# Moving transposes from TensorE to DMA in an attention and SwiGLU kernel: queries and keys of the later eight pairs, and outputs from the seventh tile on

## The chip, the cores and the metric

The kernel runs on one core of one Trainium2 chip. The metric is device time in microseconds (us), as the median of several executions. The profile is a trace of one execution; its span is about 2 us shorter than the time, because it begins with the first instruction and ends with the last. The engines are PE (TensorE matmul), PEld (its weight loads), DVE (VectorE), ACT (ScalarE), POOL (GpSimd) and SP (SyncE, which here only issues DMAs; its lines in a trace read SPq).

## The reference

Attention over 4 batches, 8 heads, 768 positions and 64 dimensions. Three heads (0, 2, 6) are causal; five see only a window of 64 positions and 4 sink positions. A SwiGLU block on 3072 rows of 512 follows.

```python
scores = scale * np.matmul(q, k.transpose(0, 1, 3, 2))
stream_keep = causal & (is_sink | in_win)
scores = np.where(mask[None, :, :, :], scores, -1000000000.0)
a = np.exp(scores - max);  a = a / (sum(a) + 1e-09)
attn_out = np.matmul(a, v)
# ...
x = attn_out.transpose(0, 2, 1, 3).reshape(B * S, H * D)     # 3072 x 512
g = x @ w_gate                                               # 512 x 1536
silu = g * (1.0 / (1.0 + np.exp(-g)))
return (silu * (x @ w_val)) @ w_out                          # 1536 x 512
```

## The kernel before

The 3072 rows are 24 tiles of 128; two tiles in succession make a "pair", for which 256 positions of q, k and v are loaded in three DMAs of 512 KB. There are twelve pairs, 0 to 11. Four tiles make a "group" for the SwiGLU block, six in all. While PE runs the gate and value matmuls of one group, it runs the attention of the next in between, so the block gives PE steady work and the attention must be ready in time.

Everything is cast to 16 bits by ACT, DVE or POOL. Scores need the head dimension on the partitions, so queries and keys are transposed by PE against an identity, into PSUM, and copied out; the attention output `xb` goes the same way into `xt`, and from tile 12 on by a DMA.

```python
RINGS = {"raw": 11, "hq": 2, "e": 7, "xb": 3, "xt": 2, "sig": 2, "sil": 3, ...}   # buffers
XBAR = 12

def cast(n, kd, j):                       # q or k of pair n, one half of the positions
    ...
    copy(T_c[n, kd, j], hqs[n][:, "qk".index(kd), j]..., r[:, :, j]...)

def transposes(n, w):                     # w = 0: queries, 1: keys; 8 matmuls each
    ...
    for j in range(2):
        for p in range(4):
            nc.tensor.transpose(tr[...], hqs[n][:, w, j, p // 2, ...], ident)

def evack(n, x, ps):                      # PSUM -> SBUF
    copy(T_ev[n, 2][x], kT[b % 2][:, ps, pi * 256:(pi + 1) * 256], trs[n, 1][:, ps]...)

def xtranspose(t):
    if t >= XBAR:
        nc.sync.dma_start_transpose(out=xts[g][:, :, n * 128:(n + 1) * 128], in_=xb...)
        return
    # ... else four PE transposes and a copy
```

Each piece of work is a task. Two long strings, `ORDER` and `WAYS`, fix the order of all tasks and the engine of each; every engine, and the sync queue as well, runs its own list strictly in that order. An instruction that is not ready therefore holds up everything behind it on its engine. All loads and DMA transposes, and all stores but the last, are issued by the sync queue.

The softmax here doesn't subtract the row's maximum and nothing guards it: scores larger than these inputs give would overflow.

## Time and profile before

| | before |
|---|---|
| time | 271.59 us (271.56 to 271.64, 4 runs) |
| span, mean granted PE clock | 269.7 us, 1.000 |
| first gate matmul of group 2 starts | 73.5 us |
| last matmul ends | 265.1 us |
| DMA moved on the main queues | 36.05 MB |

The page cuts the span into 40 slices of 6.7 us and prints the busy share of each in tenths.

```profile
PE   7799889899999999999999999999999999999993
PEclk9999999999999999999999999999999999999999
DMA  7999999999950999011114210102014220110144
```

PE is full from the ninth slice on, its clock was never lowered, and the DMA engines are 90% busy or more only in slices 2 to 11 and 14 to 16. Two groups of instructions on the page are what the change acts on: the PE transposes of queries and keys, and the DMA transposes of outputs at the page's end (2.4 us from issue to landing).

```profile
L413 PE MATMUL tr<-ident,hq 128*128 128x128 f16 x192 | 15.0, 219 | 2.1 <-DVE m L264 1.0
```

The columns are busy us and mean ns of one, then the engine's idle time before them. The 219 ns includes the pipeline; in a row they start every 56 ns.

### The profile page before, as it was taken

Reading aid. Unit: us, or ns where it says so; the run is one execution under the profiler, and the core shown is the slowest. Engines: PE = TensorE matmul, PEld = TensorE weight load, DVE = VectorE, ACT = ScalarE, POOL = GpSimd, SP = SyncE. Lnnn points to the kernel's source line nnn. Section 1 sums busy time; section 2 is a strip of 40 time slices with the busy share of each in tenths; the row PEclk is TensorE's granted clock in tenths of the full one; section 3 lists DMA queues with packets and bytes.
Section 4 is the critical chain, followed back from the end, with each engine's and each line's share of the span. In section 5 each row is a group of like instructions: output and inputs, shape, how many; then the busy total and the mean of one; then the engine's idle time right before and its main releaser. Section 6 shows DMA issues by size and latency. Waiting matters only on the chain.

```text
span 269.7 us, 5353 instructions
## 1 busy us (share of the span) xinstructions
PE 257.9 (96%) x2063; PEld 150.2 (56%) x2063; DVE 173.6 (64%) x340; ACT 167.1 (62%) x260; POOL 113.0 (42%) x145
## 2 busy tenths in 40 slices
PE   7799889899999999999999999999999999999993
PEld 7777546465655565455566655555555554444441
DVE  6757787896679487666668257764582565555321
ACT  2499779999897668767757974486564613141300
POOL 6679936774786541876523233366320200000000
PEclk9999999999999999999999999999999999999999
DMA  7999999999950999011114210102014220110144
GB/s 193 295 347 349 332 280 357 341 288 290 289 158 11 256 310 277 8 40 41 39 21 98 61 39 19 41 19 62 1 23 96 59 59 3 39 39 0 41 102 93
DMA packets 55801, 36.52 MB, mean 135 GB/s; under 512 B 8160, under 2 KB 51168, under 8 KB 55776
## 3 DMA queue, kind: packets, MB, share of 16 engines
q1 hardware_dynamic: 55696, 36.05, 50.4%
q8 instruction: 16, 0.26, 0.4%
q10 hardware_dynamic: 80, 0.13, 0.2%
q14 instruction: 9, 0.07, 0.1%
HBM read 28.31 MB, written 6.29 MB: 128 GB/s over the span
## 4 chain that ended last, share of the span: by engine, by line
PE 80%; ACT 12%; DVE 5%; issue 2%; ACTq 0%
PE gv L761 42%; PE o_ps L790 21%; PE sc L524 9%; PE av L557 5%; ACT e L540 4%; PE tr L413 3%; ACT v L178 2%; ACT hq L178 2%; ACT sig L767 1%; ACT vt L178 1%; DVE m L264 1%; PE xtr L582 1%; DVE v L290 1%; DVE k L289 1%; DVE wg_sb L180 1%
## 5 line engine op out<-in xcount | busy, mean ns | idle before, releaser
L540 ACT ACTIVATE e<-sc 128x1024 f16<-128x1024 f32 (+4 forms) x67 | 60.9, 909 | 22.9 <-PE sc L524 22.5
L761 PE MATMUL gv<-xt,wg_sb 128*128 128x512 f16 (+1 forms) x304 | 71.7, 368 | 1.7 <-DVE wg_sb L180 1.2
L761 PE MATMUL gv<-xt,wv_sb 128*128 128x512 f16 (+1 forms) x304 | 72.3, 368 | 0.0
L548 POOL TENSOR_TENSOR e<-e,m 128x640 f16<-128x640 f16 (+1 forms) x25 | 44.5, 1787 | 66.0 <-ACT e L540 65.9
L790 PE MATMUL o_ps<-wo_sb,h 128*128 128x512 f16 x288 | 71.8, 379 | 0.3 <-ACT o_sb L178 0.3
L767 ACT ACTIVATE sig<-gv 128x512 f32<-128x512 f32 (+1 forms) x76 | 43.1, 575 | 44.6 <-PE gv L761 42.6
L771 DVE SCALAR_TENSOR_TENSOR sil<-sig,gv 128x512 f32<-128x512 f32 (+1 forms) x76 | 49.5, 656 | 31.6 <-ACT sig L767 31.1
L778 DVE SCALAR_TENSOR_TENSOR h<-sil,gv 128x512 f16<-128x512 f32 (+1 forms) x76 | 48.8, 655 | 9.6 <-PE gv L761 8.5
L761 PEld LDWEIGHTS <-wg_sb 128*128 128x128 f16 x304 | 28.9, 98 | 29.3 <-DVE wg_sb L180 1.4
L761 PEld LDWEIGHTS <-wv_sb 128*128 128x128 f16 x304 | 28.7, 98 | 26.6 <-issue 0.2
L790 PEld LDWEIGHTS <-h 128*128 128x128 f16 x288 | 26.6, 98 | 26.3 <-issue 0.5
L524 PE MATMUL sc<-qT,kT 128*128 128x256 f16 (+1 forms) x228 | 35.2, 257 | 1.4 <-ACT e L540 0.8
L180 POOL COPY v<-vt 32x528 f16<-32x528 f16 (+1 forms) x46 | 29.4, 639 | 6.5 <-ACT vt L178 3.8
L524 PEld LDWEIGHTS <-kT 128*128 128x128 f16 x228 | 20.6, 98 | 13.3 <-issue 2.7
L180 POOL CAST vt<-raw 64x512 f16<-64x512 f32 x30 | 18.6, 623 | 16.1 <-DMA raw<-in_v_dram 11.2
L557 PEld LDWEIGHTS <-e 128*128 128x128 f16 x472 | 20.1, 97 | 7.5 <-issue 0.5
L565 DVE RECIPROCAL rc<-av 128x4 f32<-128x4 f32 x48 | 8.6, 180 | 24.0 <-PE av L557 23.6
L178 ACT CAST hq<-raw 128x512 f16<-128x512 f32 x32 | 19.3, 617 | 4.3 <-DMA raw<-in_q_dram 3.0
L557 PE MATMUL av<-vt,e 128*128 128x65 f16 x392 | 21.7, 193 | 0.2 <-DVE xb L566 0.2
L566 DVE TENSOR_TENSOR xb<-av,rc 128x256 f16<-128x256 f32 x48 | 20.4, 424 | 1.7
L413 PE MATMUL tr<-ident,hq 128*128 128x128 f16 x192 | 15.0, 219 | 2.1 <-DVE m L264 1.0
L413 PEld LDWEIGHTS <-hq 128*128 128x128 f16 x192 | 12.2, 98 | 5.7 <-DVE m L264 1.2
(57 smaller groups left out, 191.8 us busy)
## 6 DMA issues: line engine op xcount, KB each, us to landing
raw<-in_q_dram SPq DMA_DIRECT2D x12, 512.0 KB, 7.2
raw<-in_k_dram SPq DMA_DIRECT2D x12, 512.0 KB, 7.1
raw<-in_v_dram SPq DMA_DIRECT2D x12, 512.0 KB, 7.4
out_dram<-o_sb SPq DMA_DIRECT2D x47, 128.0 KB, 2.3
raw<-in_moe_w_gate_dram SPq DMA_DIRECT2D x6, 512.0 KB, 8.7
raw<-in_moe_w_val_dram SPq DMA_DIRECT2D x6, 512.0 KB, 8.7
raw<-in_moe_w_out_dram SPq DMA_DIRECT2D x6, 512.0 KB, 7.5
xt<-xb SPq DMA_TRANSPOSE x12, 2.4
```

The lines of the kernel that those rows point to most:

```text
L178: nc.scalar.copy(out=dst, in_=src)
L180: ENG[task.way[0]].tensor_copy(out=dst, in_=src)
L413: nc.tensor.transpose(tr[:, p, :, j, :] if w else tr[:, j, p, :], hqs[n][:, w, j, p // 2, (p % 2) * 128:(p % 2 + 1) * 128], ident)
L524: nc.tensor.matmul(sc[c // 4][:, c % 4:c % 4 + n, :], weights, moving, start=first, stop=last)
L540: nc.scalar.activation(out=e[:, 0:n], in_=whole_sc.pop((t, u))[:, 0:n], func=AF.Exp, scale=scale)
L548: ENG[task().way[0]].tensor_tensor(out=ev, in0=ev, in1=mm, op=ALU.mult)
L557: nc.tensor.matmul(av[:, n, 0:65], ee, vv, start=(m == 0), stop=(m == len(bl) - 1))
L761: nc.tensor.matmul(ps, wsb[:, kk, j * 128:(j + 1) * 128], xt[:, kk, c[0]:c[1]], start=(kk == 0), stop=(kk == 3))
L767: nc.scalar.activation(out=sg[g, j, c], in_=gs[g, j, c], func=AF.Tanh, scale=0.5)
L771: nc.vector.scalar_tensor_tensor(out=sl[g, j, c], in0=sg.pop((g, j, c)), scalar=1.0, op0=ALU.add, in1=gs.pop((g, j, c)), op1=ALU.mult)
L778: nc.vector.scalar_tensor_tensor(out=hs[g, j][:, c[0]:c[1]], in0=sl.pop((g, j, c)), scalar=0.5, op0=ALU.mult, in1=vs.pop((g, j, c)), op1=A ...
L790: nc.tensor.matmul(o_open[g, tt], hs[g, j][:, tt * 128:(tt + 1) * 128], wo_sb[:, j, :], start=(j == 0), stop=(j == NJ - 1))
```

## The change

The intent is to take work off PE, which is the bound. For pairs 4 to 11 a DMA writes transposed queries and keys straight into `qT` and `kT`; the outputs of tiles 6 to 11 join those that a DMA already transposed. The two heads of a query pair must end up in separate columns with zeros in the other's rows, so queries are first cast into a zero-filled tile `hqz` twice as wide. The start is rearranged too (smaller score units, halved first weight casts, other load order), the ring of exponential tiles `e` has six buffers instead of seven, and the two strings are made anew.

```diff
-    XBAR = 12
+    XBAR = 6
+    XQK = 4
+    hqz = const.tile([128, 2, 2, 4, 128], FH, name="hqz")
 def cast(n, kd, j):
+        if n >= XQK and kd == "q":
+            for s_ in range(2):
+                copy(T_c[n, kd, j], hqz[:, j, s_]...[:, :, :, s_ * 64:(s_ + 1) * 64], ...)
+            return
+    def dmaq(n, j):                                     # 128 partitions x 1024 columns
+        nc.sync.dma_start_transpose(
+            out=qT[n % 2][:, :, :, j].rearrange("c s p n -> c (s p) n"),
+            in_=hqz[:, j].rearrange("p s a x -> p (s a x)"))
+    def dmak(n, j):                                     # twice 64 partitions x 512 columns
+        b, pi = QP[n]
+        for m in range(2):
+            at = pi * 256 + m * 128 + j * 64
+            nc.sync.dma_start_transpose(
+                out=kT[b % 2][:, :, at:at + 64],
+                in_=hqs[n][m * 64:(m + 1) * 64, 1, j].rearrange("p r x -> p (r x)"))
     # ... tasks dq{n}.{j}, dk{n}.{j} in place of tr/evq/evk where n >= XQK
     # ... ORDER, WAYS and the first tiles' score units replaced
```

So each of the eight pairs brings two query transposes of 256 KB and four key transposes of 64 KB to the sync queue: with the six outputs, 54 issues.

## The prediction

> **What bounds the kernel now.** I first read the page's busy shares and its chain, which is followed back from the last instruction.
>
> ```profile
> PE 257.9 (96%) x2063; PEld 150.2 (56%) x2063; DVE 173.6 (64%) x340; ACT 167.1 (62%) x260; POOL 113.0 (42%) x145
> ...
> PE 80%; ACT 12%; DVE 5%; issue 2%; ACTq 0%
> ```
>
> TensorE (PE) is busy 96% of the span and carries 80% of the chain. Busy time of pipelined matmuls does not prove that the array streams without gaps, so I took the real pace from the chain in order of time, where matmuls follow one another.
>
> ```profile
> 98.99 0.45 PE tr L413 x8
> ...
> 239.21 6.04 PE gv L761 x28
> ...
> 253.02 12.10 PE o_ps L790 x56
> 265.14 0.59 ACT o_sb L800
> 265.76 0.69 DVE o_sb L801
> ```
>
> The reader sees three prices: eight transposes take 0.45 us (0.056 each), a 512-column matmul takes 6.04/28 = 0.216 us. By columns, I price 256 columns at 0.109, 384 at 0.163 and the 65-column value matmul at 0.0295 us (its group in the trace starts every 30 ns). The last matmul ends at 265.1 us, and 4.6 us of copies and store follow.
>
> Then I cut the span into stretches at the first gate matmul (22.1 us), the first output projection (58.4) and the first gate matmul of the second group of four tiles (73.5).
>
> ```profile
> 0.00:22.10 22.10, 18.81 (x261) 16.63 (x262) 15.09 (x34) 13.24 (x21) 15.21 (x38) 1.00 1.02 284
> 22.10:58.40 36.30, 32.76 (x294) 21.11 (x292) 29.64 (x60) 32.15 (x52) 26.73 (x34) 1.00 1.11 326
> 58.40:73.50 15.10, 14.67 (x156) 9.37 (x155) 10.63 (x25) 13.53 (x21) 8.55 (x13) 1.00 1.11 287
> 73.50:265.10 191.60, 191.60 (x1359) 103.13 (x1357) 117.56 (x223) 107.57 (x167) 62.46 (x63) 1.00 0.30 71
> ```
>
> The columns are PE, its weight loads, DVE, ACT, POOL (busy us and count), PE clock, DMA share, GB/s. After 73.5 us nothing but PE is near full. I counted the matmuls of the built program from that gate on: 480 + 252 of 512 columns, 128 of 256, 55 + 96 + 16 of 128, 330 of 65. At the prices above that is 191.0 us, against 191.6 measured. So this stretch has **no slack**: every PE microsecond removed there comes off the time. Before 73.5 us the same count gives only 51.2 us of useful PE work. There the limits are ACT (32.2 of 36.3 us), DVE (29.6) and the DMA engines (share 1.0 or more up to 73.5 us), chained through one another.
>
> **What the Trainium skill says.** (1) "TensorE: Matmul & The Clock Gate", section "Part 4: PE-mode transpose": a PE transpose puts its output in PSUM, so a copy must follow, and one measured about 275 ns in a kernel. The trace has 219 ns for one alone but 56 ns each in a row; the row is what counts here. (2) "Advanced Engine Details and Errata", section "X-Bar Transpose (TRN2)": "TRN2 transpose DMAs are as fast as regular DMAs". The trace agrees where DMA is quiet: a transpose of 128 KB lands in 2.4 us, a store of 128 KB in 2.3. A single one at 166 us uses a share of 0.16 of 4 us, so 0.64 us of all engines. (3) "DMA: Bandwidth & Descriptors", section "Queues, rings and completion order": each DMA engine consumes descriptors in ring order. The trace agrees, and this is the danger of the change:
>
> ```profile
> xt<-xb SPq DMA_TRANSPOSE x12, 2.4
> ...
> out_dram<-o_sb SPq DMA_DIRECT2D x47, 128.0 KB, 2.3
> ...
> L814 SPq DMA_DIRECT2D out_dram<-o_sb x2: 590/1144/1697, 93.5 to 95.3; - x2
> DMA to landing us min/median/max: 5.5/6.2/6.9
> ```
>
> The last two lines are the tile view of the output between 90 and 96 us: two stores issued right behind five 512 KB loads took 5.5 and 6.9 us. The twelve transposes of the kernel before all come after 129 us, when no load is left; in the new one the first come among the loads.
>
> **The change part by part.** *Removed from PE:* 8 pairs x 16 transposes = 128, and 6 tiles x 4 = 24; 152 x 0.056 = 8.5 us. The count of the two built programs agrees: before the first gate matmul of the second group 51.2 us becomes 51.0 (three output projections more stand there, so fewer later), and after it 191.0 becomes 182.7. *Removed from the copying engines:* for these pairs 15 copies on DVE x 0.688 and 9 on ACT x 1.004, so 10.3 and 9.0 us, and six output copies x 0.417 = 2.5 us of DVE. Most of it lies beside PE work after 73.5 us, where it gains nothing.
>
> *Added:* the query casts split in two, because zeros must lie between the halves; six of 16 go to POOL. I charge 0.2 us for each second instruction, about 3 us in sum, also hidden. On the DMA side come 16 query transposes of 256 KB, 32 key transposes of 64 KB and 6 of 128 KB. By bytes at 0.64 us for 128 KB that is 16 x 1.28 + 32 x 0.32 + 6 x 0.64 = 34.6 us of the 16 engines (an estimate), most of it where the share is 0.3 or where loads now spread out. The sync queue gets 54 issues; at the 1.19 us of such an issue in the trace that is about 65 us more in a queue that stands in order.
>
> *Moved:* the start. Tiles 0 and 1 use smaller score units and more banks, first weight casts are halved, copies are split, pair 2's loads come before most weights. Useful PE work before the second group is unchanged, but in the built order DVE sheds before that gate two weight casts (1.94 and 1.50 us in the trace), four of eight output copies (4 x 0.417) and two mask products (about 0.75 each): some 6.6 us. ACT and POOL stay about as they are. The last weights of the first group are the 29th to 31st loads. At the trace's pace of 1.55 us a load the 31st lands near 52.5 us; its cast takes 1.0, and 12.9 us of PE work remain to the second group: 66.5 us at best. DMA transposes of pairs 4 and 5 and tiles 6 and 7 now sit just before that point behind loads; tile 7's has 2.2 us of PE work between its issue and its use, while one behind loads may take 5 to 7. I choose **70 us** for the start of the second group (73.5 before).
>
> *The sum:* 70.0 + 182.7 + 0.6 (191.6 less 191.0, kept) = 253.3. Waits for the last transpose at the start of later groups: those of tiles 11, 15, 19 and 23 are followed by only 1.5, 2.2, 2.6 and 1.7 us of PE work, against 2.4 to land; I allow 2.3 us in all, with some delay behind loads for pairs 6 to 9. Then 4.6 for the tail, and 1.9 for what the time has over the span (271.56 - 269.7): **262.0 us**, 3.5% less.
>
> **Rivals.** *A wait takes the removed work's place.* Between the second and third group the sync queue must issue eight loads and most of the query and key transposes. If loads slow its issues (they took 1.5 to 2 us each at 90 to 104 us), scores come late and PE waits 1 to 2 us at each of several pairs. For it speaks the store behind loads; against it that most key and query transposes are issued 4 to 20 us of PE work ahead. It would give 265 to 269. *The start gains more.* If the DVE relief and the earlier queries show fully, the second group starts near 67 and the time is 258 to 259. *The start hides everything or loses.* If ACT, whose work up to there hardly changes, sets the start, the second group stays at 73.5 and the time is about 265.5. *Transposes hidden but PE not the bound.* The full stretch of 191.6 us against 191.0 of work speaks against it; it would leave the time near 271.
>
> **Range and chances.** The PE saving of 8.5 us is nearly sure; the start moves the time by -3.5 to +3.5 around my choice, the DMA waits by -2 to +5. That gives 257.5 to 268.0. The limit for faster by 2% is 266.1: chance 0.80, within 2% 0.17, slower 0.03.
>
> **What would show it.** PE matmul count down by 152 besides warming ones (138 for 156). The first gate of the second group near 70 us, then about 185 us to the last matmul. Gaps of 1 to 3 us of PE before the first gates of groups, released by a DMA into the output tile. Transposes at 60 to 105 us landing in 3 to 7 us, later ones in 2.4. Wrong would be: a gate at 73.5 or later, PE idle for over 6 us in sum after it, or query transposes of far over 2 us issue time that back up the sync queue.

## The result, and the profile after

| | before | after |
|---|---|---|
| time | 271.59 us | **284.61 us** (284.25 to 284.97, 4 runs) |
| span, mean PE clock | 269.7, 1.000 | 282.5, 0.978 |
| first gate of group 2 | 73.5 | 82.65 |
| from there to the last matmul's end | 191.6 | 195.25 |

The changed kernel is slower: the ratio is 1.048, with a 95% interval of 1.046 to 1.050. A ratio here is the mean time of one kernel's fast runs over that of the other's in the same rounds, so it is not quite the ratio of the medians in the tables. Of the span's 12.8 us more, 9.15 came before the second group and 3.65 after its first gate. First the page: shares, slices, and the shares of the chain.

```profile
PE 254.1 (90%) x1893; PEld 143.9 (51%) x1893; DVE 161.3 (57%) x322; ACT 164.9 (58%) x267; POOL 113.1 (40%) x152
...
PE   8999989976489996789999979999999999999993
...
PEclk9999999997869999999999999999999999999998
...
PE 63%; DMA 16%; ACT 7%; POOL 4%; DVE 3%; issue 3%; SPq 2%; POOLq 0%; ACTq 0%; DVEq 0%
```

The work did leave PE: 170 matmuls fewer, 18 of them warming ones. But PE fell from 96% to 90% of the span, there are holes in slices 9 to 12 and 16 to 18, the clock drops in the first of them, and the chain now runs through DMAs for 16% of the span, where there was none. The stretches have the columns of the prediction's last view of the kernel before:

```profile
58.40:82.65 24.25, 15.84 (x119) 8.76 (x118) 7.08 (x18) 12.77 (x22) 6.05 (x9) 0.79 1.02 218
82.65:277.90 195.25, 185.60 (x1241) 96.22 (x1239) 111.52 (x208) 103.04 (x165) 61.97 (x72) 1.00 0.47 103
```

Between 58.4 us and the second group all four engines are idle for long: PE works 15.8 of 24.3 us at a clock of 0.79, POOL 6.1. Something that is none of them is being waited for. PE's timeline shows the two large holes; the brackets give the idle time before the line and what the profile believes ended it.

```profile
65.95 0.59 PE L580 MATMUL sc<-qT,kT 128*128 128x256 f16 x2 [3.52 <-ACT e L590]
...
78.58 0.37 PE L580 MATMUL sc<-qT,kT 128*128 128x256 f16 x1 [4.79 <-issue]
```

ACT's timeline tells what stood behind both.

```profile
64.27 0.71 ACT L180 CAST hqz<-raw 128x256 f16<-128x256 f32 x2 [3.17 <-DMA qT<-hqz]
...
78.56 0.71 ACT L180 COPY k<-kT 128x256 f16<-128x256 f16 x2 [5.85 <-DMA kT<-hq]
```

The exponentials before the first hole were late because ACT, whose list is fixed, stood at the query cast of pair 5: it may not overwrite `hqz` before pair 4's transposes have read it. The second hole ends on PE (78.58) and on ACT (78.56) with one landing at 78.5 us: keys of pair 4, in a transpose issued at 73.09 that took 5.4 us to land. The list of those who waited for `kT` names the victims, us and times:

```profile
  POOL k L182: 24.2, 5
...
  ACT k L180: 8.3, 3
  DVE hq L182: 7.1, 3
...
  PE sc L580: 4.8, 1
```

Now the sync queue itself. Each line is start, duration of the issue, instruction and how many in succession.

```profile
57.69 4.49 SPq L435 DMA_TRANSPOSE qT<-hqz  x2
62.27 1.19 SPq L910 DMA_DIRECT2D out_dram<-o_sb  x2
63.51 0.58 SPq L327 DMA_DIRECT2D raw<-in_v_dram  x1
64.15 0.66 SPq L327 DMA_DIRECT2D raw<-in_q_dram  x1
64.85 1.34 SPq L327 DMA_DIRECT2D raw<-in_k_dram  x1
66.29 3.77 SPq L443 DMA_TRANSPOSE kT<-hq  x2
70.10 0.58 SPq L327 DMA_DIRECT2D raw<-in_v_dram  x1
70.74 2.24 SPq L327 DMA_DIRECT2D raw<-in_q_dram  x1
73.09 2.47 SPq L443 DMA_TRANSPOSE kT<-hq  x2
76.07 2.59 SPq L637 DMA_TRANSPOSE xt<-xb  x2
```

There is hardly a moment between one issue and the next. Pair 4's keys had been cast by 61 us; their transposes were issued at 66.3 and 73.1 us because the queue had other things to do, and PE needed the result at 73.8. I added up the issues that start between 57.5 and 99.2 us, each by its own duration: 17 transposes take 25.7 us, 10 loads 8.3 and 8 stores 5.4, so 39.4 of 41.7 us. In the kernel before, the same stretch holds 16 loads and 8 stores, 30.0 us, and one wait of 10.3 us. The tile views give the duration of one issue (minimum, median, maximum in ns):

```profile
L443 SPq DMA_TRANSPOSE kT<-hq x32: 1185/1246/2476, 66.3 to 167.8; - x32
L435 SPq DMA_TRANSPOSE qT<-hqz x16: 1232/1273/3465, 57.7 to 196.0; - x16
L637 SPq DMA_TRANSPOSE xt<-xb x18: 1189/1210/2219, 76.1 to 238.9; - x18
```

In the median, a transpose of 64 KB, one of 128 KB and one of 256 KB each hold the queue about 1.2 us; among loads a single one took up to 3.5. A load of 512 KB with nothing in its way holds it 0.58 us (63.51 above). That leads to the theory: **the sync queue's time per transpose issue, in a queue that works in order, is what the change adds to the path.** The rivals: the single `hqz` buffer; an unlucky order of the queue; the bytes and the traffic on the DMA engines; or the rearranged start itself.

### The profile page after: what moved, and what is told of

It reads as the page before. It is cut to its first block, busy times and chain, and to the rows that moved or that the text cites. A ratio compares the mean times of both kernels' runs of the same rounds, so it can differ in the third digit from the quotient of the medians.

```text
span 282.5 us, 5129 instructions
## 1 busy us (share of the span) xinstructions
PE 254.1 (90%) x1893; PEld 143.9 (51%) x1893; DVE 161.3 (57%) x322; ACT 164.9 (58%) x267; POOL 113.1 (40%) x152
## 3 DMA queue, kind: packets, MB, share of 16 engines
q1 hardware_dynamic: 85072, 43.14, 62.8%
## 4 chain that ended last, share of the span: by engine, by line
PE 63%; DMA 16%; ACT 7%; POOL 4%; DVE 3%; issue 3%; SPq 2%; POOLq 0%; ACTq 0%; DVEq 0%
PE gv L857 32%; PE o_ps L886 18%; PE sc L580 7%; DMA raw<-in_moe_w_out_dram 6%; PE av L610 4%; DMA raw<-in_q_dram 3%; ACT e L590 3%; DMA xt<-xb 3%; DMA qT<-hqz 2%; PE warm L302 2%; DMA kT<-hq 2%; POOL e L598 1%; ACT v L180 1%; SPq L443 1%; DVE m L267 1%
## 5 line engine op out<-in xcount | busy, mean ns | idle before, releaser
L590 ACT ACTIVATE e<-sc 128x1024 f16<-128x1024 f32 (+4 forms) x71 | 62.1, 880 | 28.9 <-PE sc L580 28.3
L857 PE MATMUL gv<-xt,wg_sb 128*128 128x512 f16 (+1 forms) x304 | 70.3, 368 | 4.4 <-DMA xt<-xb 3.8
L857 PE MATMUL gv<-xt,wv_sb 128*128 128x512 f16 (+1 forms) x304 | 70.5, 368 | 0.2
L598 POOL TENSOR_TENSOR e<-e,m 128x640 f16<-128x640 f16 (+1 forms) x25 | 42.8, 1718 | 49.7 <-ACT e L590 47.8
L580 PE MATMUL sc<-qT,kT 128*128 128x256 f16 (+1 forms) x228 | 36.3, 260 | 15.0 <-ACT e L590 9.7
L182 POOL CAST vt<-raw 64x512 f16<-64x512 f32 x26 | 16.3, 628 | 33.9 <-DMA raw<-in_v_dram 26.8
L182 POOL COPY v<-vt 2x528 f16<-2x528 f16 (+1 forms) x40 | 25.4, 635 | 1.8
L180 ACT COPY o_sb<-o_ps 128x512 f32<-128x512 f32 x14 | 8.2, 585 | 20.3 <-PE o_ps L886 11.9
L615 DVE RECIPROCAL rc<-av 128x4 f32<-128x4 f32 x48 | 8.6, 179 | 19.6 <-PE av L610 19.3
L180 ACT CAST hq<-raw 128x512 f16<-128x512 f32 x24 | 14.6, 620 | 7.6 <-DMA kT<-hq 3.2
L180 ACT COPY v<-vt 32x528 f16<-32x528 f16 (+1 forms) x24 | 15.1, 629 | 0.4
```

The source lines that it names most:

```text
L180: nc.scalar.copy(out=dst, in_=src)
L182: ENG[task.way[0]].tensor_copy(out=dst, in_=src)
L580: nc.tensor.matmul(sc[c // 4][:, c % 4:c % 4 + n, :], weights, moving, start=first, stop=last)
L590: nc.scalar.activation(out=e[:, 0:n], in_=whole_sc.pop((t, u))[:, 0:n], func=AF.Exp, scale=scale)
L598: ENG[task().way[0]].tensor_tensor(out=ev, in0=ev, in1=mm, op=ALU.mult)
L857: nc.tensor.matmul(ps, wsb[:, kk, j * 128:(j + 1) * 128], xt[:, kk, c[0]:c[1]], start=(kk == 0), stop=(kk == 3))
```

## The experiments

All twelve kernels gave correct results and were timed beside the kernel before on the same chip (medians 271.44 to 271.48 us; two chips in all, of which the second ran the small transposes and the last three kernels of the table). "Start" is the first gate of group 2.

| run | time, us (range) | ratio to before (95%) | start, us |
|---|---|---|---|
| changed kernel | 284.61 (284.25-284.97) | 1.048 (1.046-1.050) | 82.65 |
| two `hqz` buffers | 284.11 (282.71-285.79) | 1.047 (1.042-1.051) | 82.4 |
| transposes first in the queue | 292.14 (290.61-292.97) | 1.075 (1.071-1.080) | 80.6 |
| no q/k DMA transposes | 280.68 (280.17-281.59) | 1.034 (1.031-1.037) | 72.9 |
| outputs by DMA from tile 12 | 277.96 (276.16-279.15) | 1.025 (1.021-1.029) | 78.6 |
| q/k by DMA from pair 6 | 278.59 (278.24-281.19) | 1.028 (1.023-1.033) | 74.0 |
| wide keys | 272.84 (272.24-273.64) | 1.006 (1.003-1.009) | 76.9 |
| wide keys, 16 small transposes more | 284.03 (282.95-284.31) | 1.046 (1.043-1.048) | 78.9 |
| wide keys, outputs from 12 | 273.31 (272.45-274.04) | 1.006 (1.004-1.009) | 75.5 |
| wide keys, outputs from 12, two `hqz` | 274.34 (271.42-275.41) | 1.008 (1.001-1.016) | 74.9 |
| wide keys, outputs from 8 | 274.20 (272.85-275.60) | 1.010 (1.006-1.015) | 73.4 |
| wide keys, pair 6 on | **268.68** (268.26-269.43) | 0.990 (0.988-0.993) | 73.0 |
| wide keys, pair 6 on, outputs from 8 | 271.80 (270.88-272.88) | 1.001 (0.998-1.005) | 73.4 |

A caution on the last column: it comes from one profiled execution each. Eight of these kernels (the changed one among them) have the same sync queue up to the first query transpose, at which the trace shows 55.6 to 57.7 us, since loads land a little earlier or later; the changed kernel is the latest of them. So a start carries about 2 us of chance, and differences of the whole time, with four runs each, are the safer measure.

### Two buffers for the query casts

```diff
-    hqz = const.tile([128, 2, 2, 4, 128], FH, name="hqz")
+    hqz = [const.tile([128, 2, 2, 4, 128], FH, name=f"hqz{n}") for n in range(2)]
-        [T_fill3] + T_dq.get(n - 1, []) if free else []
+        [T_fill3] + T_dq.get(n - 2, []) if free else []
     # and 16-bit "sig" and "sil" tiles, for room
```

> The changed kernel with two buffers for the zero-padded queries instead of one (room for it made by keeping the two SwiGLU intermediates in 16 bits). Theory A, the single buffer: the query cast of the next pair waits in ACT's and POOL's in-order streams until both transposes of the pair before have read the buffer, and the exponentials behind it wait too. Then the waits of ACT and POOL on those transposes (8.8 us in sum) vanish, the PE gap of 3.5 us before 66 us and that of 2.1 us before 112 us vanish, and the time falls from 284.6 to 275 to 278. Theory B, the sync queue: transposes are issued late because that queue takes them in order among loads, and the next wait, on the keys, takes over; the time stays above 282. Theory C, the new start of the kernel: nothing changes, 284.

The hole at 66 us closed to 0.24 us, and the time stayed. On PE's timeline of this run the next hole had grown instead:

```profile
78.22 0.37 PE L581 MATMUL sc<-qT,kT 128*128 128x256 f16 x1 [7.40 <-issue]
```

3.52 and 4.79 us had become 0.24 and 7.40, and PE got the keys within 0.4 us of the moment in the changed kernel. The hole of 2.1 us at 112 us, which theory A expected to vanish, was now one of 4.71 us at 118 us. The buffer is a wait that comes before a worse one; taking it away only moves PE's waiting.

### Transposes ahead of loads and stores in the queue

Only the order of the sync queue differs; the part around the hole:

```diff
-  dq4.0 dq4.1 st Lx5 Lq6 Lk6 dk4.0 Lx6 Lq7 dk4.1 xdma6 xdma7
+  dq4.0 Lk5 dq4.1 st dk4.0 Lx5 dk4.1 Lq6 Lk6 xdma6 Lx6 Lq7 xdma7
```

> The changed kernel with only the order of the sync queue altered: every transpose moves ahead of the loads and stores that stood between it and the last thing it depends on. Theory B: the keys of pair 4 then land before 72 us instead of 78.5, the PE gap of 4.8 us before 78.6 us shrinks to under 1, and the time falls from 284.6 to 276 to 280. Theory A: the gap before 66 us and the wait of ACT on the query buffer stay, the time stays above 282. Theory C: 284.

The keys' hole is gone, but the first gate of group 2 then waited for its outputs:

```profile
80.62 4.46 PE L857 MATMUL gv<-xt,wg_sb 128*128 128x512 f16 x12 [6.16 <-DMA xt<-xb]
```

Later a hole of 5.76 us opened at 135.7 us, where PE waited for ACT's output copy, which waited for a store that now stood behind transposes. The kernel got 7.5 us slower, which was not foreseen: theory B expected 276 to 280, and the others a time about where it was. This is only one other order, and it was made by hand; that no order of the same issues would do well is not shown. It does show that a transpose which moves forward pushes back what stood before it.

### Queries and keys back on PE

```diff
-    XQK = 4
+    XQK = NP          # never; PE transposes and copies stand at the places of the DMA tasks
-    RINGS hq: 2
+    RINGS hq: 3       # hqz is not needed
```

> The changed kernel with queries and keys of the later eight pairs transposed on PE again, at the places where their DMAs stood (128 PE transposes, 7.2 us of PE work, and their copies come back); the start and the DMA transposes of outputs stay. Theories A and B: PE's gaps between 60 and 170 us go, the granted clock is 1.00, and the time is 266 to 272. Theory C, the new start as the cause: the second group still begins after 78 us and the time stays above 280.

```profile
72.90 2.76 PE L857 MATMUL gv<-xt,wg_sb 128*128 128x512 f16 x12 [1.15 <-DMA xt<-xb]
```

The start came 9.75 us earlier than in the changed kernel, of which 1.7 were there before the first transpose, so the query and key transposes cause some 8 us of the late start. The run also bounds the rearranged start: without those DMAs it stands at 72.9, against 73.5 before, a gain of 0.6 us. (The last kernel of the table, in which no transpose at all goes by DMA before that gate, stands at 73.4.) The total missed its expectation by over 8 us. The stretch took 200.9 us for 189.0 us of PE work (the count of its built program at the prediction's prices): the copies that came back stand at places where nobody had tuned them, and PE has many holes under 1.2 us. As a measure of the whole time this run is no clean reversal; as one of the start it is.

### Outputs of tiles 6 to 11 back on PE

```diff
-    XBAR = 6
+    XBAR = 12
```

> The changed kernel with the outputs of tiles 6 to 11 transposed on PE again (24 PE transposes, 1.3 us, and six copies come back). Theories A and B: only the waits of the gates on those outputs go (1.5 us before the third group), so 283 to 285. If the output transposes of the loading phase were the cause, or crowded out the key transposes: 279 or less.

Theories A and B expected far too small a gain: it gave 6.6 us, although PE has more to do. What came true is the last branch, 279 or less: outputs that crowd out the key transposes. The second group starts 4 us earlier, but 1.5 of these were there before any issue that differs. What does differ is the queue after pair 4's keys: the changed kernel issued two output transposes at 76.1 us and the next load at 78.7; here that load goes out at 74.0 us, 4.7 us earlier, and everything behind it moves with it. The miss speaks for the queue: the cost of an issue is paid by whatever stands behind it.

### The same key bytes in half as many transposes

This is the run meant to separate issues from bytes. The keys are cast so that one DMA of 64 partitions by 1024 columns can replace two of 512; `kT` is laid out anew for that. The bytes on the queues stay at 43.14 MB; key issues fall from 32 to 16. Each key cast becomes two instructions. A transpose now waits for both halves of the keys, so the first key transposes of pairs 8, 10 and 11 also stand later in the queue than in the changed kernel.

```diff
-    kT = [const.tile([128, 4, S], FH, ...)]
+    kT = [const.tile([128, NT // 2, 2, 4, 2, 64], FH, ...)]
     def dmak(n, j):
-        for m in range(2):
-            at = pi * 256 + m * 128 + j * 64
-            nc.sync.dma_start_transpose(out=kT[b % 2][:, :, at:at + 64],
-                in_=hqs[n][m * 64:(m + 1) * 64, 1, j]...)
+        nc.sync.dma_start_transpose(
+            out=kT[b % 2][:, pi, j].rearrange("c p i n -> c (p i) n"),
+            in_=hqs[n][j * 64:(j + 1) * 64, 1].rearrange("p i r x -> p (i r x)"))
```

> The changed kernel with the keys of a pair transposed by two DMAs of 1024 columns from 64 partitions instead of four of 512, into a key layout that allows it (each key cast becomes two instructions, about 0.2 us more each). Bytes and DMA rows are the same, the sync queue issues 16 transposes fewer. Theory B1, the issue time of the sync queue: each transpose takes 1.2 us there whatever its size, so 16 x 1.25 = 20 us leave the queue, the second group starts at 74 to 78 us instead of 82.6, and the time is 272 to 278. Theory C1, the DMA engines themselves, shared by loads and transposes: the bytes are the same, so the time stays at 281 to 285.

The time fell by 11.8 us to 272.84. The first fence is the tile view of `kT` in this run, the second PE's timeline, the third the stretch from there (columns as above).

```profile
L448 SPq DMA_TRANSPOSE kT<-hq x16: 1194/1270/3452, 64.9 to 155.3; - x16
```

```profile
76.88 2.76 PE L862 MATMUL gv<-xt,wg_sb 128*128 128x512 f16 x12 [2.10 <-DMA xt<-xb]
```

```profile
76.88:265.70 188.82, 184.91 (x1240) 96.32 (x1240) 111.53 (x213) 105.82 (x177) 62.84 (x72) 1.00 0.51 110
```

A transpose of twice the size takes the queue 1.27 us for 1.25. All transposes together held the queue for 91.4 us in the changed kernel and hold it for 71.8 here, 19.6 us less. The start gained 5.8 us (1.7 of them before the first key transpose) and the stretch 6.4, for the same PE work (182.7 us) and more casts. Bytes and their traffic cannot be what cost those 11.8 us: the bytes are the same, and the packets of the main queues took the DMA engines no less time (62.8% of 282.5 us = 177 us there, 66.7% of 270.3 = 180 here).

### Sixteen small transposes on top

The counter-test: the wide-key kernel, with the issues put back as transposes that carry almost nothing. All else in the order of the queue is that of the kernel with wide keys, so the three moved transposes are no rival here.

```diff
+    spare = [const.tile([128, 64], FH, name=f"spare{n}") for n in range(2)]
     def dmak(n, j):
         ...
+        nc.sync.dma_start_transpose(out=spare[j], in_=hqs[n][j * 64:(j + 1) * 64, 1, 0, 0, 0:128])
```

> The kernel with wide key transposes (272.8 us) plus one more transpose after each of its 16: 64 partitions by 128 columns, 16 KB, an eighth of the bytes, into a spare tile that nothing reads. Theory B1, issue time of the sync queue: if a small transpose also takes about 1.2 us of the queue, the 20 us saved come back and the time returns to 279 to 286. Theory C1, the DMA engines: 6% more transposed bytes, 272 to 275. If the small ones issue in under 0.4 us, B1 expects about 273 to 275 and this run decides nothing.

The little transposes move 16 KB each, 0.26 MB or 0.6% of the bytes together. Their tile view, and PE at the start of group 2:

```profile
L452 SPq DMA_TRANSPOSE spare<-hq x16: 1179/1226/1233, 67.9 to 170.4; - x16
```

```profile
78.87 4.45 PE L864 MATMUL gv<-xt,wg_sb 128*128 128x512 f16 x12 [3.70 <-DMA xt<-xb]
```

An eighth of a key transpose's bytes takes the queue 1.23 us all the same, and the kernel is back at 284.03, 11.2 us slower, for 16 x 1.23 = 19.6 us of queue time. The loss does not lie where the gain lay: the start is 2.0 us later, and the rest came after it. Holes of 3.7 and 2.9 us opened at 111 and 151 us, and the clock fell with them. The slices of the PE clock, first the wide-key kernel, then this one:

```profile
PEclk9999999998999999999999999999999999999999
```

```profile
PEclk9999999997979998799997999999999999999998
```

One impurity: the small transpose reads the cast keys, so their buffer is free only when it too has landed. Casts into that buffer waited 12.1 us for the small ones here, and 4.5 us for key transposes in the wide-key kernel; those are waits of DVE and ACT, not of PE. With this run, halving the issues and doubling them back move the time by the same 11 to 12 us in either direction while bytes hardly change. I take the cost of an issue as shown for this queue.

### Fewer pairs by DMA, and combinations

```diff
-    XQK = 4
+    XQK = 6           # narrow keys: the changed kernel; wide keys: the kernel with wide keys
```

> The changed kernel with DMA transposes of queries and keys from pair 6 on only; pairs 4 and 5, whose transposes fell among the last loads and weights, go through PE (32 transposes, 1.8 us). Theories B1 and C1 both: the second group starts near 73 us (72.9 with none by DMA) and the clock stays at 1.0 there, the gaps at 112 to 117 us stay: 274 to 279. If the harm is spread evenly over all eight pairs: 281 or more.

> Wide key transposes, and DMA transposes of queries and keys from pair 6 on only (pairs 4 and 5 through PE, 1.8 us of PE work). What is left of the loss with wide keys is the start of the second group (76.9 against 73.5 before), so this should bring it to 73 to 74 and the time to 268 to 271. If something other than pairs 4 and 5 holds the start, it stays near 76 and the time at 273 to 275.

Pairs 4 and 5 are the ones whose DMAs stand among loads around the start of the second group. With them back on PE, the narrow form gained 6.0 us over the changed kernel (start 74.0, then holes near 2 us at 105, 110 and 146 us), and the wide form 4.2 us over wide keys. The wide form is the best kernel of all, 1.0% faster than the one before; its interval lies wholly below 1. Its PE timeline, stretch and clock:

```profile
73.03 2.76 PE L862 MATMUL gv<-xt,wg_sb 128*128 128x512 f16 x12 [1.36 <-DMA xt<-xb]
```

```profile
73.03:262.10 189.07, 185.68 (x1256) 97.14 (x1256) 112.07 (x213) 104.37 (x172) 62.97 (x72) 1.00 0.49 105
```

The stretch has 183.6 us of PE work, 7.4 less than before, and takes 189.07: 5.5 us are still waits, where the kernel before had 0.6. About 2.5 us of the saving in the stretch survive, and 0.5 at the start.

I then tried to take still more issues away from the queue.

```diff
-    XBAR = 6
+    XBAR = 12         # or 8; with wide keys; once with two hqz buffers; once with XQK = 6
```

> As the run before, and the outputs of tiles 6 to 11 go through PE again (which alone gave 278.0). Theory B1: both take issues off the same queue, so the gains add in good part: 266 to 273, and key transposes of pair 4 land before 74 us. Theory C1: 276 to 279, as with the outputs alone.

> As the run before, with two buffers for the zero-padded queries. If the single buffer is a wait hidden behind that of the queue (alone its doubling gave nothing), it now counts: 2 to 4 us less than the run before. If not, the same within 1 us.

> As the run before, and the outputs of tiles 6 and 7 through PE too, so that no transpose goes by DMA before the second group; the gate that waited 1.5 to 2.1 us for the last of them no longer does. 266 to 270, the start of the second group at 71 to 73 us. If the weights' arrival and ACT hold that start, it does not move: 268 to 271.

> Wide key transposes with only the outputs of tiles 6 and 7 back on PE, queries and keys of all eight pairs by DMA. The gate's wait of 2.1 us goes: 270 to 272. If the wait moves to the keys or queries of pair 4, which share the queue: 272 to 274, as when all of tiles 6 to 11 went back (273.3).

None of them helped, and all of these expectations were at least partly missed. With wide keys, outputs back on PE from tile 12 or 8 start the second group earlier (75.5 and 73.4 for 76.9) and lose it again later: in the last of these runs a hole of 2.65 us follows at 78.8 us. With pair 6 on and outputs from 8 there are holes of 2.05 us at 104.6 us and 1.06 us at 119.5 us, the second before a DMA into `xt`. So the two reliefs do not add. Once the queue has room, the returned transposes and copies seem to cost as much as the issues they save, in an order not tuned for them; what exactly, I did not isolate.

## Why the prediction was wrong, point by point

Its sum was 70.0 + 185.6 + 4.6 + 1.9 = 262.1 us, which it gives as 262.0. Measured, the first term is 82.65 (+12.65) and the second 195.25 (+9.65); the last two were right. 262.1 + 12.65 + 9.65 = 284.4, the profiled execution took 284.25.

- **What bounds the kernel before, and PE's saving: right.** 152 matmuls fewer and 182.7 us of work in the stretch, as counted. The step from "no slack" to "every PE microsecond removed there comes off the time" was not: new waits took the place of the work. The copying engines' relief is there as well (DVE 161.3 us busy for 173.6); the time shows nothing of it. A small misreading: the 219 ns of a transpose are the mean of all 192, not of one alone.
- **The step that failed** is the sum's treatment of this sentence: "The sync queue gets 54 issues; at the 1.19 us of such an issue in the trace that is about 65 us more in a queue that stands in order." The count and the price were right: 32 x 1.25 + 16 x 1.27 + 6 x 1.21 = 67.6 us. But the 65 us were never laid against the room in the queue in the stretch where they fall, and no term of the sum holds them; only "the DMA waits by -2 to +5" does. Together with the mis-sized start (below), those waits are the 22 us. Of the 41.7 us from 57.5 us on, the queue of the kernel before already used 30.0 for loads and stores, so some 12 us were free where 17 transposes had to go: 20 us at 1.19, and 25.7 as measured. Those are numbers that the trace of the kernel before, the built order and the 1.19 us would have given.
- **The argument that closed the door** was "most key and query transposes are issued 4 to 20 us of PE work ahead". That is their place in the program. Pair 4's keys were cast by 61 us and issued at 66.3 and 73.1; the lead was used up by standing in the queue.
- **The start at 70 us** was mis-sized even without the queue. With no query and key DMAs it is 72.9 us, so the rearrangement is worth 0.6 us, not 3.5. So the relief of DVE moved it little. This is 2.9 of the 12.65 us; the other 9.75 came with the query and key transposes, less the 1.7 us by which that execution was ahead before them.
- **The rival "A wait takes the removed work's place" named the right mechanism**, a sync queue that delays scores, and gave it 265 to 269 us, where 284.6 came. It thought of loads that slow the issues. The larger part is that every transpose costs 1.2 us of the queue with no load in its way, whatever its size. The text's other fear, "query transposes of far over 2 us issue time", was wrong for most: their median is 1.27, the longest took 3.5.
- **Landing times were nearly right**: 4.4 to 7.5 us for pair 4's keys among loads (3 to 7 predicted), 2.3 to 4.4 for all issued after 105 us (2.4 predicted). So were the gaps before gates that wait for outputs: 1.5 and 1.9 us at 127 and 165 us.
- **Not foreseen at all** was the clock. The trace shows 1.00 before. Here, in stretches of 2 us, it is 0.50 from 66 to 68 us and from 76 to 82 us, with the changes inside the stretches beside these. The Trainium skill has the rule in "TensorE: Matmul & The Clock Gate", section "Why this matters for your kernels": "No PE-idle gaps >~3µs between matmul bursts". The trace agrees that the holes of 3.5 and 4.8 us are followed by half the clock. From those stretches I estimate that PE worked at half clock for some 2.9 us after the first hole and 3.9 after the second, so 3.4 us were lost to slower matmuls, inside the 22. No run separates the clock from the waits that lower it.

What stays open: how much the clock costs alone, whether another order of the same 54 issues could hide them, whether loads and stores issued by another engine would make room in the sync queue (no run tried it), and why outputs on PE do not help beside wide keys.

## What to carry to other kernels

In these runs a DMA was paid for in three places: its bytes, its time to land, and the time its issue holds the queue. Moving work to DMA needs a budget for the third: sum the issues per stretch, and compare with what is left of the queue there. Where transposes can be merged at the same bytes, merge them (11.8 us here for 16 issues fewer); and look first at those that stand among loads (4.2 us more when the two pairs there went back to PE; fewer issues and a better place are not separated by that run).

## What the Trainium skill lacked or had wrong

- "Advanced Engine Details and Errata", section "X-Bar Transpose (TRN2)", says that transposes are as fast as regular DMAs. That held for the landing (2.4 us for 128 KB, as a store of that size) and not for the issue: 1.2 to 1.3 us of the sync queue in the median, against 0.58 for an unhindered load of 512 KB. The page has no issue time of a transpose, and no page has a measured one for transposes from SBUF to SBUF on this chip.
- "DMA: Bandwidth & Descriptors", section "Rules for kernel authors", advises to coalesce small transfers, since "under 64 KB you're paying mostly overhead". For the issue of SBUF-to-SBUF transposes the runs show no such limit: 16, 64, 128 and 256 KB took 1.23, 1.25, 1.21 and 1.27 us of queue time in the median, so up to 256 KB size made hardly any difference to it.
- "TensorE: Matmul & The Clock Gate", same section as above: about 3 us as the longest harmless hole is too much. In the kernel with wide keys, a single hole of 2.46 us that ended at 64.5 us was followed by a clock of 0.50 from 66 to 68 us. Nor does the length alone decide: with pair 6 on and outputs from 8, a hole of 2.05 us that ended at 104.6 us was followed by 0.50 from 106 to 108 us, while after one of 2.10 us that ended at 76.9 us with wide keys the clock stayed at 1.00.
